# One decode step of attention plus FFN on one core: bias row, uneven last weight chunks, FFN behind attention, fewer K buffers

The chip is one Trainium2, the kernel runs on one NeuronCore. The metric is the device time of one execution in microseconds (us), median of several runs.

Names in what follows: PE multiplies matrices (PEld is the loading of its weights) and writes to PSUM; DVE and ACT are the vector and the scalar engine, POOL is GpSimd; SyncE (SP) issues loads; a q behind a name (SPq) marks what an engine's instruction queue does. A load has landed when the last of the 16 DMA engines has reported its share.

## The reference

For one token `x` (512 values) the kernel computes a layernorm, then two branches, and adds them to `x`:

```python
xn = layernorm(x)                                   # 1 x 512
q  = xn @ wq                                        # 512 x 4096: 32 heads of 128
k, v = last 1024 positions of the caches            # 32 heads x 1024 x 128, bf16
o  = softmax(q k^T * 128**-0.5) v
A  = o @ wo                                         # 4096 x 512
h  = relu(xn @ w1 + b1)**2                          # 512 x 1376
B  = h @ w2 + b2                                    # 1376 x 512
out = x + A + B
```

All of it is matrix times vector. K, V, wq, wo, w1 and w2 are read once, 27.99 MB in all by the page's count of reads, and nothing is used twice.

## The kernel before

SyncE issues all large loads in one queue, in the order wq, K, w1, w2, V, wo. ACT's queue takes the small ones. (Cuts are marked with `...`.)

```python
    b2T = const.tile([P, DJ], BF16, name="b2T")                    # P = 128, DJ = 4
    with nc.allow_non_contiguous_dma(reason="tiny b2 transpose load"):
        nc.scalar.dma_start(out=b2T[:], in_=B_b2.rearrange("(c p) -> p c", p=P))
    ...
    for g in range(NHG):                                           # 8 K tiles of 1 MB, then w1, w2, 8 V tiles
        kg = kvpool.tile([P, HG, NB, DH], BF16, name="kg", tag="k4", bufs=NHG)
        ...
    for q in range(NWC):                                           # 4 chunks of wo, 8 row blocks each
        woq = wpool.tile([P, JQ, D], BF16, name="woq", tag="w8k", bufs=NWC)
        nc.sync.dma_start(out=woq[:], in_=...)                     # rows of 512 bf16: 1 KB pieces
    ...                                                            # layernorm, then hT (FFN), q, K loop, softmax, V
    for q in range(NWC):
        ...
        for c in range(DJ):
            if q == 0: ...                                         # w2 matmuls into the same PSUM tile
            for jj in range(JQ):
                nc.tensor.matmul(oq[:, c:c + 1], lhsT=woq[:, jj, c * P:(c + 1) * P], rhs=oT_sb[:, j:j + 1], ...)
        ...                                                        # acc += oq, for q == 1 also acc += b2T
    nc.vector.tensor_copy(out=outT_bf[:], in_=acc[:])
    for c in range(DJ):
        nc.tensor.matmul(row_ps[0:1, c * P:(c + 1) * P], lhsT=outT_bf[:, c:c + 1], rhs=ident[:, :], start=True, stop=True)
    nc.vector.tensor_copy(out=out_sb[:], in_=row_ps[:])
    nc.scalar.dma_start(out=out[0, 0:1, :], in_=out_sb[:])
```

## Time and profile before

| | before |
|---|---|
| device time | 84.87 us (6 runs, 84.72 to 85.15) |
| span of the profiled run | 83.07 us |
| last byte of wo landed | 78.21 us |
| from there to the end of the span | 4.86 us |
| DMA queue of SyncE, share of the 16 engines | 93.0% |
| busiest compute engine | PE, 60% |

The span is what the profile covers; the device time is some 1.9 us longer. The way to read this table is: a stream of loads that never stops, then a short serial tail. The lines behind it stand in the prediction.

Two kinds of line need a key. A line of a timeline gives start and length in us, engine, line of the kernel, operation, output<-inputs, shapes and count; in brackets, how long the engine was idle before it and what ended that. A line of a stretch gives its bounds and length, the busy time of PE, PEld, DVE, ACT and POOL (with counts), the granted clock of PE (1.00 is full), the busy share of the DMA engines (above 1 where packets overlap) and GB/s.

### The profile page before, as it was taken

What the parts mean: (1) busy time and instruction counts of PE and PEld (TensorE: products, weight loads), DVE (VectorE), ACT (ScalarE), POOL (GpSimd) and SP (SyncE); (2) the same over time, 40 slices, a digit from 0 to 9 for tenths busy, and PEclk for the clock granted to TensorE, in tenths of its full rate; (3) what the DMA queues carried; (4) which work ended last, traced back from release to release, by engine and by line L of the source; (5) the groups of instructions that cost most, each with busy time, mean ns of one, the idle gap of its engine ahead of it and who ended that gap; (6) DMA issues with size and microseconds to landing.
All of it is one profiled execution on the core that took longest, in us unless ns stands there. A gap on an engine that the chain in (4) does not pass through costs nothing.

```text
span 83.1 us, 2488 instructions
## 1 busy us (share of the span) xinstructions
PE 50.2 (60%) x1149; PEld 45.3 (55%) x1149; DVE 20.5 (25%) x49; ACT 15.4 (19%) x17; POOL 0.8 (1%) x7
## 2 busy tenths in 40 slices
PE   0120001999898879896798929911791881564340
PEld 0120001999798768775697818901791871564320
DVE  0131000014533545363535620163100000020040
ACT  0634000004043144143440440014000000000000
POOL 4000000000000000000000000000000000000000
PEclk9999999999999999999999996555555555555555
DMA  2799998999999999999999999999999999999100
GB/s 28 320 427 407 406 351 257 400 398 388 387 390 387 383 388 388 387 394 386 353 360 386 387 389 379 387 387 387 390 384 380 363 348 347 350 348 293 61 8 0
DMA packets 15664, 28.15 MB, mean 339 GB/s; under 512 B 963, under 2 KB 6437, under 8 KB 15142
## 3 DMA queue, kind: packets, MB, share of 16 engines
q1 hardware_dynamic: 15008, 27.89, 93.0%
q10 hardware_dynamic: 646, 0.10, 0.8%
q8 instruction: 9, 0.15, 0.8%
q14 instruction: 1, 0.01, 0.0%
HBM read 27.99 MB, written 0.00 MB: 337 GB/s over the span
## 4 chain that ended last, share of the span: by engine, by line
PE 41%; DMA 29%; ACT 10%; DVE 9%; issue 7%; SPq 1%; ACTq 0%; DVEq 0%
DMA wqj<-in_A_wq_dram 14%; PE kt_ps L166 14%; DMA woq<-in_A_wo_dram 14%; ACT kT L169 9%; PE scT_ps L173 7%; PE oT_ps L204 7%; DVE kT L171 4%; PE qT_ps L155 4%; PE hT_ps L141 3%; DVE mx L182 1%; SPq L85 1%; ACT p_un L187 1%; PE hT_ps L138 1%; PE S_ps L180 1%; PE outQ L225 1%
## 5 line engine op out<-in xcount | busy, mean ns | idle before, releaser
L166 PE MATMUL kt_ps<-ident,kg 128*128 128x128 bf16 x256 | 22.1, 242 | 0.0
L171 DVE COPY kT<-kt_ps 128x1024 bf16<-128x1024 bf16 x21 | 14.0, 688 | 15.6 <-PE kt_ps L166 15.5
L166 PEld LDWEIGHTS <-kg 128*128 128x128 bf16 x256 | 17.4, 109 | 0.0
L169 ACT COPY kT<-kt_ps 128x1024 bf16<-128x1024 bf16 x11 | 11.1, 1012 | 30.5 <-PE kt_ps L166 28.4
L173 PE MATMUL scT_ps<-qT_sb,kT 128*128 128x1 bf16 x256 | 11.3, 166 | 4.5 <-ACT kT L169 3.5
L173 PEld LDWEIGHTS <-kT 128*128 128x128 bf16 x256 | 9.5, 100 | 7.2 <-ACT kT L169 4.6
L204 PE MATMUL oT_ps<-pT_sb,vg 128*128 128x1 bf16 x256 | 7.1, 165 | 2.5 <-issue 2.0
L155 PE MATMUL qT_ps<-xnT,wqj 128*128 128x1 bf16 x128 | 4.0, 165 | 7.5 <-DMA wqj<-in_A_wq_dram 5.9
L204 PEld LDWEIGHTS <-vg 128*128 128x128 bf16 x256 | 7.0, 104 | 2.7 <-issue 2.7
L225 PE MATMUL outQ<-oT_sb,woq 128*128 128x1 bf16 x128 | 4.5, 166 | 5.8 <-DMA woq<-in_A_wo_dram 4.2
L155 PEld LDWEIGHTS <-wqj 128*128 128x128 bf16 x128 | 3.7, 104 | 7.8 <-DMA wqj<-in_A_wq_dram 6.2
L225 PEld LDWEIGHTS <-woq 128*128 128x128 bf16 x128 | 4.0, 104 | 6.1 <-DMA woq<-in_A_wo_dram 4.4
L141 PE MATMUL hT_ps<-xnT,w_sb 128*128 128x1 bf16 (+1 forms) x44 | 3.1, 175 | 0.0
L138 PE MATMUL hT_ps<-one,b_row 1*128 1x1 bf16 (+1 forms) x11 | 2.0, 185 | 1.4 <-DMA b_row<-in_B_b_dram 1.4
L158 DVE CAST qT_sb<-qT_ps 128x32 bf16<-128x32 f32 x1 | 0.2, 191 | 10.1 <-PE qT_ps L155 10.1
L207 DVE CAST oT_sb<-oT_ps 128x32 bf16<-128x32 f32 x1 | 0.2, 192 | 9.4 <-PE oT_ps L204 9.4
L195 PE MATMUL pT_ps<-ident,p_rows 32*128 32x32 bf16 x8 | 0.4, 185 | 3.5 <-DVE p_rows L192 3.5
L187 ACT ACTIVATE p_un<-S_ps,negmx 32x1024 bf16<-32x1024 bf16 x1 | 1.1, 1105 | 7.0 <-DVE negmx L184 7.0
L141 PEld LDWEIGHTS <-w_sb 128*128 128x128 bf16 (+1 forms) x44 | 2.2, 112 | 0.2
L195 PEld LDWEIGHTS <-p_rows 32*128 32x128 bf16 x8 | 0.3, 100 | 3.7 <-DVE p_rows L192 3.7
L111 PE MATMUL xT_ps<-one,x_row 1*128 1x1 bf16 x4 | 0.3, 165 | 3.2 <-DMA x_row<-in_A_x_dram 3.2
L138 PEld LDWEIGHTS <-b_row 1*128 1x128 bf16 (+1 forms) x11 | 1.1, 103 | 1.6 <-DMA b_row<-in_B_b_dram 1.5
(45 smaller groups left out, 17.9 us busy)
## 6 DMA issues: line engine op xcount, KB each, us to landing
kg<-in_A_k_cache_dram SPq DMA_DIRECT2D x8, 1024.0 KB, 14.4
vg<-in_A_v_cache_dram SPq DMA_DIRECT2D x8, 1024.0 KB, 13.9
wqj<-in_A_wq_dram SPq DMA_DIRECT2D x4, 1024.0 KB, 7.6
woq<-in_A_wo_dram SPq DMA_DIRECT2D x4, 1024.0 KB, 12.8
w_sb<-in_B_w_dram SPq DMA_DIRECT2D x1, 1376.0 KB
w_sb<-in_B_w_dram SPq DMA_DIRECT2D x1, 1280.0 KB, 16.1
w_sb<-in_B_w_dram ACTq DMA_DIRECT2D x1, 96.0 KB, 7.0
x_row<-in_A_x_dram ACTq DMA_DIRECT2D x1, 1.0 KB
```

The costliest lines, as they stand in the source:

```text
L85: nc.sync.dma_start(out=wqj[:], in_=A_wq[j * P:(j + 1) * P, :])
L138: nc.tensor.matmul(hT_ps[0:M, t:t + 1], lhsT=b1_row[0:1, t * P:t * P + M], rhs=one11[0:1, 0:1], start=True, stop=False)
L141: nc.tensor.matmul(hT_ps[0:M, t:t + 1], lhsT=w1_sb[:, j, t * P:t * P + M], rhs=xnT[:, j:j + 1], start=False, stop=(j == DJ - 1))
L155: nc.tensor.matmul(qT_ps[:, h:h + 1], lhsT=wq_tiles[j][:, h * DH:(h + 1) * DH], rhs=xnT[:, j:j + 1], start=(j == 0), stop=(j == DJ - 1))
L166: nc.tensor.transpose(kt_ps[:, b, :], kg[:, hi, b, :], ident[:, :])
L169: nc.scalar.copy(out=kT[:], in_=kt_ps[:])
L171: nc.vector.tensor_copy(out=kT[:], in_=kt_ps[:])
L173: nc.tensor.matmul(scT_ps[:, b, h:h + 1], lhsT=kT[:, b, :], rhs=qT_sb[:, h:h + 1], start=True, stop=True)
L180: nc.tensor.transpose(S_ps[:, b * P:(b + 1) * P], scT_sb[:, b, :], ident[:, :])
L187: nc.scalar.activation(out=p_un[:], in_=S_ps[:], func=ACT.Exp, bias=negmx[:], scale=1.0, accum_out=ssum[:])
L204: nc.tensor.matmul(oT_ps[:, h:h + 1], lhsT=vg[:, hi, b, :], rhs=pT_sb[:, b, h:h + 1], start=(b == 0), stop=(b == NB - 1))
L225: nc.tensor.matmul(oq[:, c:c + 1], lhsT=woq[:, jj, c * P:(c + 1) * P], rhs=oT_sb[:, j:j + 1], start=first, stop=(jj == JQ - 1))
```

## The change

It follows the habits of someone tuning the end and the small loads: load b2 as one row and add it by a matmul; cut wo so that the last chunk is short; let the last add write bf16; copy the result on ACT and send it from SyncE; put the FFN behind attention in the source with its own PSUM tile; take six K buffers and three kT buffers to make room for the longer wo chunks.

```diff
-    NWC = 4
+    WO_CHUNKS = [10, 10, 9, 3]
+    NWBIG = 4
+    K_BUFS = 6
...
-    b2T = const.tile([P, DJ], BF16, name="b2T")
-    with nc.allow_non_contiguous_dma(reason="tiny b2 transpose load"):
-        nc.scalar.dma_start(out=b2T[:], in_=B_b2.rearrange("(c p) -> p c", p=P))
+    b2_row = const.tile([1, D], BF16, name="b2_row")
+    nc.scalar.dma_start(out=b2_row[:], in_=B_b2.rearrange("(o f) -> o f", o=1))
...                                   (hT, relu: moved from ahead of q to behind oT)
-        kT = work.tile([P, NB, P], BF16, name="kT", tag="kT", bufs=4)
+        kT = work.tile([P, NB, P], BF16, name="kT", tag="kT", bufs=3)
...
+    outB = psum.tile([P, DJ], F32, name="outB", tag="PH")          (w2 matmuls go here)
+    nc.vector.tensor_add(out=acc[:], in0=xcat[:, 0:DJ], in1=outB[:])
...
-    nc.vector.tensor_copy(out=outT_bf[:], in_=acc[:])
+        nc.vector.tensor_add(out=(outT_bf if last else acc)[:], in0=acc[:], in1=oq[:])
+    nc.tensor.matmul(row_ps[:, :], lhsT=one11[0:1, 0:1], rhs=b2_row[0:1, :], start=True, stop=False)
...
-    nc.vector.tensor_copy(out=out_sb[:], in_=row_ps[:])
-    nc.scalar.dma_start(out=out[0, 0:1, :], in_=out_sb[:])
+    nc.scalar.copy(out=out_sb[:], in_=row_ps[:])
+    nc.sync.dma_start(out=out[0, 0:1, :], in_=out_sb[:])
```

More of the change, by code (lines that the diff above doesn't have):

```diff
@@ L48 @@
     NOQ = HQ * DH // P
-    NWC = 4
-    JQ = NOQ // NWC
-    NDQ = DH // 32
-    assert NDQ * 32 == DH and HQ == 32
+    WO_CHUNKS = [10, 10, 9, 3]
+    NWBIG = 4
     KT_BUFS = 4
+    K_BUFS = 6
+    V_BUFS = 8
     const = ctx.enter_context(tc.tile_pool(name="const", bufs=1))
@@ L77, with bigdma @@
     nc.scalar.dma_start(out=w2_sb[0:FLAST, FT - 1, :], in_=B_w2[(FT - 1) * P:F, :])
-    b2T = const.tile([P, DJ], BF16, name="b2T")
-    with nc.allow_non_contiguous_dma(reason="tiny b2 transpose load"):
-        nc.scalar.dma_start(out=b2T[:], in_=B_b2.rearrange("(c p) -> p c", p=P))
+    b2_row = const.tile([1, D], BF16, name="b2_row")
+    nc.scalar.dma_start(out=b2_row[:], in_=B_b2.rearrange("(o f) -> o f", o=1))
+    qengines = [nc.sync]
+    qi = [0]
+    def bigdma(out_ap, in_ap):
+        eng = qengines[qi[0] % len(qengines)]
+        qi[0] += 1
+        eng.dma_start(out=out_ap, in_=in_ap)
     wq_tiles = []
     for j in range(DJ):
-        wqj = wpool.tile([P, HQ * DH], BF16, name="wqj", tag="w8k", bufs=NWC)
-        nc.sync.dma_start(out=wqj[:], in_=A_wq[j * P:(j + 1) * P, :])
+        wqj = wpool.tile([P, HQ * DH], BF16, name="wqj", tag="wbig", bufs=NWBIG)
+        bigdma(wqj[:], A_wq[j * P:(j + 1) * P, :])
         wq_tiles.append(wqj)
@@ L88 @@
     for g in range(NHG):
-        kg = kvpool.tile([P, HG, NB, DH], BF16, name="kg", tag="k4", bufs=NHG)
+        kg = kvpool.tile([P, HG, NB, DH], BF16, name="kg", tag="k4", bufs=K_BUFS)
         src = A_k_cache[0, g * HG:(g + 1) * HG, SK - W:SK, :].rearrange("h (p b) d -> p h b d", b=NB)
-        nc.sync.dma_start(out=kg[:], in_=src)
+        bigdma(kg[:], src)
         k_tiles.append(kg)
-    nc.sync.dma_start(out=w1_sb[:], in_=B_w1.rearrange("(j p) f -> p j f", p=P))
-    nc.sync.dma_start(out=w2_sb[:, 0:FT - 1, :],
-                      in_=B_w2[0:(FT - 1) * P, :].rearrange("(t p) n -> p t n", p=P))
+    bigdma(w1_sb[:], B_w1.rearrange("(j p) f -> p j f", p=P))
+    bigdma(w2_sb[:, 0:FT - 1, :], B_w2[0:(FT - 1) * P, :].rearrange("(t p) n -> p t n", p=P))
     v_tiles = []
     for g in range(NHG):
-        vg = kvpool.tile([P, HG, NB, DH], BF16, name="vg", tag="v4", bufs=NHG)
+        vg = kvpool.tile([P, HG, NB, DH], BF16, name="vg", tag="v4", bufs=V_BUFS)
         src = A_v_cache[0, g * HG:(g + 1) * HG, SK - W:SK, :].rearrange("h (p b) d -> p h b d", b=NB)
-        nc.sync.dma_start(out=vg[:], in_=src)
+        bigdma(vg[:], src)
         v_tiles.append(vg)
     wo_tiles = []
-    for q in range(NWC):
-        woq = wpool.tile([P, JQ, D], BF16, name="woq", tag="w8k", bufs=NWC)
-        nc.sync.dma_start(out=woq[:],
-                          in_=A_wo[q * JQ * P:(q + 1) * JQ * P, :].rearrange("(j p) n -> p j n", p=P))
-        wo_tiles.append(woq)
+    j0 = 0
+    for q, nj in enumerate(WO_CHUNKS):
+        if nj >= 8:
+            woq = wpool.tile([P, nj, D], BF16, name="woq", tag="wbig", bufs=NWBIG)
+        else:
+            woq = wpool.tile([P, nj, D], BF16, name="wolast", tag=f"wosmall{q}", bufs=1)
+        bigdma(woq[:], A_wo[j0 * P:(j0 + nj) * P, :].rearrange("(j p) n -> p j n", p=P))
+        wo_tiles.append((j0, nj, woq))
+        j0 += nj
+    assert j0 == NOQ
     xT_ps = psum.tile([P, DJ], F32, name="xT_ps", tag="PA")
@@ L133 @@
                             op0=ALU.subtract, op1=ALU.mult)
-    hT_ps = psum.tile([P, FT], F32, name="hT_ps", tag="PH")
-    for t in range(FT):
-        M = P if t < FT - 1 else FLAST
-        nc.tensor.matmul(hT_ps[0:M, t:t + 1], lhsT=b1_row[0:1, t * P:t * P + M], rhs=one11[0:1, 0:1],
-                         start=True, stop=False)
-        for j in range(DJ):
-            nc.tensor.matmul(hT_ps[0:M, t:t + 1], lhsT=w1_sb[:, j, t * P:t * P + M], rhs=xnT[:, j:j + 1],
-                             start=False, stop=(j == DJ - 1))
-    h_bf = work.tile([P, FT], BF16, name="h_bf")
-    h2 = const.tile([P, FT], BF16, name="h2")
-    nc.vector.tensor_copy(out=h_bf[:, 0:FT - 1], in_=hT_ps[:, 0:FT - 1])
-    nc.vector.scalar_tensor_tensor(out=h2[:, 0:FT - 1], in0=h_bf[:, 0:FT - 1], scalar=0.0, in1=h_bf[:, 0:FT - 1],
-                                   op0=ALU.max, op1=ALU.mult)
-    nc.vector.tensor_copy(out=h_bf[0:FLAST, FT - 1:FT], in_=hT_ps[0:FLAST, FT - 1:FT])
-    nc.vector.scalar_tensor_tensor(out=h2[0:FLAST, FT - 1:FT], in0=h_bf[0:FLAST, FT - 1:FT], scalar=0.0,
-                                   in1=h_bf[0:FLAST, FT - 1:FT], op0=ALU.max, op1=ALU.mult)
     qT_ps = psum.tile([P, HQ], F32, name="qT_ps", tag="PA")
@@ L207 @@
     nc.vector.tensor_copy(out=oT_sb[:], in_=oT_ps[:])
+    hT_ps = psum.tile([P, FT], F32, name="hT_ps", tag="PH")
+    for t in range(FT):
+        M = P if t < FT - 1 else FLAST
+        nc.tensor.matmul(hT_ps[0:M, t:t + 1], lhsT=b1_row[0:1, t * P:t * P + M], rhs=one11[0:1, 0:1],
+                         start=True, stop=False)
+        for j in range(DJ):
+            nc.tensor.matmul(hT_ps[0:M, t:t + 1], lhsT=w1_sb[:, j, t * P:t * P + M], rhs=xnT[:, j:j + 1],
+                             start=False, stop=(j == DJ - 1))
@@ new lines @@
+    h_bf = work.tile([P, FT], BF16, name="h_bf")
+    h2 = const.tile([P, FT], BF16, name="h2")
+    nc.vector.tensor_copy(out=h_bf[:, 0:FT - 1], in_=hT_ps[:, 0:FT - 1])
+    nc.vector.scalar_tensor_tensor(out=h2[:, 0:FT - 1], in0=h_bf[:, 0:FT - 1], scalar=0.0, in1=h_bf[:, 0:FT - 1],
+                                   op0=ALU.max, op1=ALU.mult)
+    nc.vector.tensor_copy(out=h_bf[0:FLAST, FT - 1:FT], in_=hT_ps[0:FLAST, FT - 1:FT])
+    nc.vector.scalar_tensor_tensor(out=h2[0:FLAST, FT - 1:FT], in0=h_bf[0:FLAST, FT - 1:FT], scalar=0.0,
+                                   in1=h_bf[0:FLAST, FT - 1:FT], op0=ALU.max, op1=ALU.mult)
@@ L209 @@
+    outB = psum.tile([P, DJ], F32, name="outB", tag="PH")
+    for c in range(DJ):
+        for t in range(FT):
+            Kt = P if t < FT - 1 else FLAST
+            nc.tensor.matmul(outB[:, c:c + 1], lhsT=w2_sb[0:Kt, t, c * P:(c + 1) * P], rhs=h2[0:Kt, t:t + 1],
+                             start=(t == 0), stop=(t == FT - 1))
     acc = const.tile([P, DJ], F32, name="acc")
-    out_tags = ["PA", "PB", "KT", "KT"]
-    for q in range(NWC):
+    nc.vector.tensor_add(out=acc[:], in0=xcat[:, 0:DJ], in1=outB[:])
@@ L212 @@
+    outT_bf = work.tile([P, DJ], BF16, name="outT_bf")
+    out_tags = ["PA", "PB", "KT", "KT", "KT", "KT"]
+    for q, (j0, nj, woq) in enumerate(wo_tiles):
         oq = psum.tile([P, DJ], F32, name=f"outQ{q}", tag=out_tags[q],
                        bufs=(KT_BUFS if out_tags[q] == "KT" else 1))
-        woq = wo_tiles[q]
         for c in range(DJ):
-            first = True
-            if q == 0:
-                for t in range(FT):
-                    Kt = P if t < FT - 1 else FLAST
-                    nc.tensor.matmul(oq[:, c:c + 1], lhsT=w2_sb[0:Kt, t, c * P:(c + 1) * P], rhs=h2[0:Kt, t:t + 1],
-                                     start=first, stop=False)
-                    first = False
-            for jj in range(JQ):
-                j = q * JQ + jj
-                nc.tensor.matmul(oq[:, c:c + 1], lhsT=woq[:, jj, c * P:(c + 1) * P], rhs=oT_sb[:, j:j + 1],
-                                 start=first, stop=(jj == JQ - 1))
-                first = False
@@ L228 @@
-        if q == 0:
-            nc.vector.tensor_add(out=acc[:], in0=xcat[:, 0:DJ], in1=oq[:])
-        else:
-            nc.vector.tensor_add(out=acc[:], in0=acc[:], in1=oq[:])
-        if q == 1:
-            nc.vector.tensor_add(out=acc[:], in0=acc[:], in1=b2T[:])
-    outT_bf = work.tile([P, DJ], BF16, name="outT_bf")
-    nc.vector.tensor_copy(out=outT_bf[:], in_=acc[:])
+            for jj in range(nj):
+                j = j0 + jj
+                nc.tensor.matmul(oq[:, c:c + 1], lhsT=woq[:, jj, c * P:(c + 1) * P], rhs=oT_sb[:, j:j + 1],
+                                 start=(jj == 0), stop=(jj == nj - 1))
@@ L237 @@
+        last = q == len(wo_tiles) - 1
+        nc.vector.tensor_add(out=(outT_bf if last else acc)[:], in0=acc[:], in1=oq[:])
     row_ps = psum.tile([1, D], F32, name="row_ps", tag="PA")
+    nc.tensor.matmul(row_ps[:, :], lhsT=one11[0:1, 0:1], rhs=b2_row[0:1, :], start=True, stop=False)
     for c in range(DJ):
         nc.tensor.matmul(row_ps[0:1, c * P:(c + 1) * P], lhsT=outT_bf[:, c:c + 1], rhs=ident[:, :],
-                         start=True, stop=True)
+                         start=False, stop=(c == DJ - 1))
```

## The prediction

> **What bounds the kernel now.** I read the page's slices first, then the busy time by stretch, then the tail of the timeline, then what the DMA queue of SyncE waited for.
>
> ```profile
> PE 50.2 (60%) x1149; PEld 45.3 (55%) x1149; DVE 20.5 (25%) x49; ACT 15.4 (19%) x17; POOL 0.8 (1%) x7
> ...
> DMA  2799998999999999999999999999999999999100
> GB/s 28 320 427 407 406 351 257 400 398 388 387 390 387 383 388 388 387 394 386 353 360 386 387 389 379 387 387 387 390 384 380 363 348 347 350 348 293 61 8 0
> ...
> q1 hardware_dynamic: 15008, 27.89, 93.0%
> q10 hardware_dynamic: 646, 0.10, 0.8%
> q8 instruction: 9, 0.15, 0.8%
> ```
>
> The DMA row is full from slice 2 to slice 36, and no compute engine comes near that: the kernel is one stream of 28.15 MB on SyncE's queue plus what has to follow its last byte. Only slices 5 and 6 dip (351, 257), and slices 36 and 37 run out unevenly (293, 61). In stretches (us, then busy times; the last two columns are DMA share and GB/s):
>
> ```profile
> 3.00:10.00 7.00, 1.35 (x9) 0.99 (x9) 1.25 (x7) 2.66 (x4) 0.00 (x0) 1.00 1.02 414
> 10.00:15.00 5.00, 1.05 (x33) 0.97 (x34) 0.00 (x0) 0.00 (x0) 0.00 (x0) 1.00 0.92 316
> 15.00:35.00 20.00, 18.42 (x370) 17.16 (x368) 7.61 (x12) 5.17 (x6) 0.00 (x0) 1.00 1.05 390
> 42.00:64.00 22.00, 14.73 (x338) 13.07 (x335) 6.40 (x15) 4.23 (x5) 0.00 (x0) 0.69 1.05 384
> 66.00:76.00 10.00, 5.65 (x195) 5.35 (x193) 0.67 (x4) 0.00 (x0) 0.00 (x0) 0.50 1.10 349
> ```
>
> The wq stage runs at 414, K and V at about 390, wo at 349; 10 to 15 us is the hole. The rest of the time is the tail:
>
> ```profile
> 78.26 1.01 PE L225 MATMUL outQ<-oT_sb,woq 128*128 128x1 bf16 x32 [1.73 <-DMA woq<-in_A_wo_dram]
> 79.31 0.16 DVE L231 TENSOR_TENSOR acc<-acc,outQ 128x4 f32<-128x4 f32 x1 [2.59 <-PE outQ L225]
> 79.50 0.17 DVE L235 CAST outT_bf<-acc 128x4 bf16<-128x4 f32 x1
> ...
> 79.72 0.58 PE L239 MATMUL row_ps<-ident,outT_bf 128*1 128x128 bf16 x4 [0.45 <-DVE outT_bf L235]
> 80.35 0.68 DVE L242 CAST out_sb<-row_ps 1x512 bf16<-1x512 f32 x1 [0.68 <-PE row_ps L239]
> 81.06 0.27 ACTq L243 DMA_DIRECT2D out_dram<-out_sb  x1
> ```
>
> The last wo bytes land at 78.21 us; everything after is a serial chain of 4.86 us to the span's end at 83.07. PE waits there, before 78.26, for a transfer. So only two things count: when the stream ends, and how long the chain behind it is.
>
> **What the Trainium skill says.** (1) "DMA: Bandwidth & Descriptors", § Rules for kernel authors: a strided last dimension "lowers to one descriptor per element". The trace agrees: the b2T load of 1 KB is 512 packets of 2 bytes on ACT's queue, most of q10's 646. It was issued at 1.93 and took 13.8 us to land. (2) The same page, § Queues, rings and completion order: each DMA engine takes turns between its queues, a packet at a time. Agrees: from 7.7 to 15.2 us the packet records show about as many 2-byte starts as starts of big packets (27 and 27 in the half microsecond from 8.5). (3) The same page, § Why small descriptors are slow: a fixed cost for each packet. The stretches agree: 8 KB packets 414, 2 KB about 390, 1 KB 349 GB/s. The wo rows stay 1 KB in the change, so its stage stays at 349. (4) "Runtime: NRT & Kernel Launch", § Instruction fetch mechanics: instructions come in 16 KiB blocks of 256 through a DMA queue. Agrees: q8 has 9 packets for 0.15 MB; each takes about 1.1 us of one DMA engine. PE stalls about 2 us in mid-loop at 62.66, with no data missing, after a block was requested at 62.32.
>
> **The change, part by part.**
>
> *b2 as one row instead of b2T.* Removes the 512 tiny packets. Their own time in the packet records is 4.6 us over 16 engines: 0.29 us each, nearly sure to come back. The hole they sit in is larger: from 10 to 15 us the stream moved 316 GB/s, while about 402 (the mean of 414 and 390) would have been normal: 5 x 86 = 430 KB, at 390 GB/s 1.1 us. What I can't settle is whether they cause it all. For it: the rate is clean as soon as they end (401 to 407 GB/s from 15.1 us), K packets of 84 ns took up to 372 ns while they ran, and later changes of tensor (35, 42, 64 us) show no such hole. Against: the same mixing from 8 to 10 us cost nothing (414 GB/s). I give 0.6 that the whole 1.1 us returns, 0.4 that only 0.3 does: mean 0.8 us.
>
> The load has a second effect: SyncE's queue reuses the semaphore of b2T for the fifth K tile and waits for it:
>
> ```profile
> SPq L91 <- DMA b2T<-in_B_b_dram: 2.4, 1, 2.4
> ```
>
> That issue slips from 13.37 to 15.79 us, but the four tiles issued before it are still queued (they land at 17.4, 20.1, 22.8 and 26.8 us), so I count nothing for it.
>
> *Chunks of wo, 10+10+9+3 instead of 8 each.* The bytes are the same, so the stream's end doesn't move. Behind it stand 12 matmuls, not 32. The trace starts one each 0.027 us and the last takes 0.165: 31 x 0.027 + 0.165 = 1.01 now, 11 x 0.027 + 0.165 = 0.47 after: 0.54 off the path. The chunk before lands 3/32 of 4.19 MB, 0.39 MB, earlier: 1.1 us at 349 GB/s. Its 36 matmuls need 36 x 0.027 = 0.97 us, so they're just out of the way.
>
> *Last add writes bf16 at once.* Takes the cast L235 away: 0.17 plus 0.02 of hop, 0.19. Adding b2 as a matmul into row_ps goes ahead of the last transfer: nothing on the path. *Output copy on ACT:* kT copies on ACT take 1.01 us for 1024 columns and a one-column operation there 0.20, so 512 cost about 0.6 against 0.68: 0.08 gained. *Output DMA from SyncE:* one more of the same kind; SyncE's issues take 0.37 or more where ACT's took 0.27: 0.05 to 0.1 lost. Tail in sum: 0.54 + 0.19 + 0.08 - 0.07 = about 0.75 us.
>
> *FFN moved behind attention.* Now its hT matmuls stand among the softmax's transposes on PE (49.9 to 53.4 us) and hold the softmax up by about 3.5 us. That isn't on the path: the last V tile lands only at 66.5. If the scheduler fills PE's idle time during the softmax with them (PE idles 3.5 us before pT), oT starts near 55 instead of 58.65 and waits for V anyway. Worth 0.
>
> *Six K buffers instead of eight, three kT instead of four.* The seventh K load now waits until the first tile is transposed (head 3 ends at 21.3 us; it was issued at 19.94), the eighth until head 7 (about 26; it was 23.51). The queue holds three to four tiles of 2.7 us each, so at 26 us some three are still ahead: no gap. kT with one buffer less may add a microsecond to the K loop, which has slack until V.
>
> Sum: 0.75 of tail, 0.8 of stream: 1.55 us. 84.87 - 1.55 = 83.3.
>
> **Rivals.** *A: the hole isn't the tiny packets* (a cold start of K, or the last wq tile). Then 0.75 + 0.3 = 1.05 us: 83.8. For it speaks the clean stretch 8 to 10. *B: the FFN runs late.* If its 99 matmuls stay behind oT in PE's order, then from 67.7: hT at 0.31 us per five is 3.4 us, a relu 0.8, the second product 44 x 0.027 = 1.2, the chunks of 10, 10 and 9 rows 3.2: ready at 76.3 without a fetch stall, 78 to 80 with one or two of 2 us. PE would become the bound, for 84 to 87 us. Against it: the order of the old kernel is not that of its source (the first hT matmul runs at 5.97, the rest at 50), so instructions go where PE is free, and the new PSUM tile for the second product doesn't depend on oT. I give it one in ten. *C: K buffers starve the stream.* Would show as a hole near 27 to 35 us worth 1 to 3 us; the queue's depth speaks against it. One in twenty. *D: the uneven end stays.* The last transfer's 16 engines finished from 76.4 to 78.2: half are late by the fetches of (4). The number of PE instructions barely changes, so I expect the same 1.8 us of run-out; it is neither gain nor loss.
>
> **Range and chances.** Two humps: 84.87 - 0.75 - 1.1 = 83.0 (0.55) and 83.8 (0.33), each with about 0.25 of spread, and a thin part above 84.5 (0.12, rivals B and C, in part mild). The mean of the first two lies near 83.3. Two per cent is 1.70 us, that is 83.17, which cuts the first hump: some 0.7 of it lies below, so 0.41 faster, 0.54 same, 0.05 slower. Eight in ten: 82.7 to 84.3.
>
> **What will show each step right or wrong.** The q10 line: some 130 packets, not 646. GB/s near 390 to 410 in slices 5 and 6, and the wo transfers' end at 77.1 (rival A: 77.9). 12 matmuls behind the last landing, then one add, the row matmuls, one ACT copy near 0.6; from landing to the span's end 4.1 instead of 4.86. hT matmuls in the gap before pT and outB before oT is done. No hole between 25 and 40 us. I would be wrong if PE isn't waiting for the last transfer at the end (B), if the stream shows a new hole (C), or if the dip stands with the tiny packets gone (A).

## The result, and the profile after

The changed kernel takes 82.84 us (8 runs, 82.61 to 82.92) against 84.88 (16 runs) before; the ratio is 0.9756, with a 95% interval of 0.9744 to 0.9767: faster by 2.4%. A ratio here compares the runs of both kernels in the same rounds, so it isn't quite the ratio of the medians quoted. All runs are fast: none is more than 1% above the fastest of its kernel.

The page of the changed kernel: DMA share and GB/s in forty slices, then ACT's queue (packets, MB, share).

```profile
DMA  2799999999999999999999999999999999999400
GB/s 29 311 418 417 421 429 376 388 384 385 390 386 386 384 387 388 390 394 393 354 364 383 388 388 382 387 386 387 387 381 384 365 353 349 348 356 342 142 8 1
...
q10 hardware_dynamic: 118, 0.10, 0.5%
```

The dip of slices 5 and 6 is gone (429 and 376 now, 351 and 257 before), and ACT's queue has 118 packets instead of 646. The slow start and the uneven run-out at the end are still there. By stretch (last column GB/s):

```profile
3.00:10.00 7.00, 1.36 (x9) 0.99 (x9) 1.25 (x7) 2.28 (x4) 0.00 (x0) 1.00 1.02 423
10.00:15.00 5.00, 1.51 (x51) 1.44 (x52) 0.00 (x0) 0.00 (x0) 0.00 (x0) 1.00 1.01 400
```

From 10 to 15 us the stream moves 400 instead of 316 GB/s, and from 3 to 10 us 423 instead of 414. The last byte of wo lands at 77.00 us, 1.21 earlier. The tail in the timeline:

```profile
77.05 0.48 PE L236 MATMUL outQ<-oT_sb,wolast 128*128 128x1 bf16 x12
...
77.56 0.16 DVE L239 TENSOR_TENSOR outT_bf<-acc,outQ 128x4 bf16<-128x4 f32 x1 [0.20 <-PE outQ L236]
...
77.78 0.59 PE L244 MATMUL row_ps<-ident,outT_bf 128*1 128x128 bf16 x4 [0.25 <-DVE outT_bf L239]
78.40 0.58 ACT L247 CAST out_sb<-row_ps 1x512 bf16<-1x512 f32 x1 [23.62 <-PE row_ps L244]
79.00 0.32 SPq L248 DMA_DIRECT2D out_dram<-out_sb  x1
```

From the landing to the span's end at 81.02 us it is 4.02 us, against 4.86. So 1.21 us of the stream and 0.84 of the tail make the 2.05 us by which the spans differ. Nothing else is left to explain in the total, but two things off the path changed and are worth reading. SyncE's queue now waits for PE before the seventh and eighth K load, and V's matmuls stall twice:

```profile
SPq L87 <- PE kt_ps L160: 5.7, 2, 3.5
```

```profile
55.85 1.33 PE L224 MATMUL outB<-h,w_sb 128*128 128x1 bf16 x44
...
57.04 2.83 PE L198 MATMUL oT_ps<-pT_sb,vg 128*128 128x1 bf16 x101
...
62.06 3.58 PE L198 MATMUL oT_ps<-pT_sb,vg 128*128 128x1 bf16 x128 [2.18 <-issue]
...
68.80 0.88 PE L198 MATMUL oT_ps<-pT_sb,vg 128*128 128x1 bf16 x27 [3.17 <-issue]
```

The first is harmless: slices 12 to 18 stay at 384 to 394 GB/s. The second brings the end of oT to 69.7 us, later than before (67.8), but the second wo chunk lands only at 72.77, so PE waits for transfers again from there on.

### The profile page after: what moved, and what is told of

It is laid out like the page before. It is cut to its first block, busy times and chain, and to the rows that moved or that the text cites.

```text
span 81.0 us, 2488 instructions
## 1 busy us (share of the span) xinstructions
PE 50.0 (62%) x1150; PEld 45.1 (56%) x1150; DVE 19.5 (24%) x47; ACT 16.0 (20%) x18; POOL 0.8 (1%) x7
## 2 busy tenths in 40 slices
DMA packets 15138, 28.15 MB, mean 347 GB/s; under 512 B 436, under 2 KB 5911, under 8 KB 14616
## 3 DMA queue, kind: packets, MB, share of 16 engines
q1 hardware_dynamic: 15010, 27.89, 94.6%
## 4 chain that ended last, share of the span: by engine, by line
SPq 46%; DMA 31%; PE 17%; issue 1%; DVE 1%; ACT 1%
SPq L87 46%; DMA woq<-in_A_wo_dram 17%; DMA wqj<-in_A_wq_dram 14%; PE kt_ps L160 8%; PE qT_ps L149 4%; PE outQ L236 2%; PE scT_ps L167 1%; DVE kT L165 1%; PE row_ps L244 1%; ACT out_sb L247 1%; DVE outT_bf L239 0%
## 5 line engine op out<-in xcount | busy, mean ns | idle before, releaser
L236 PEld LDWEIGHTS <-woq 128*128 128x128 bf16 x116 | 3.4, 104 | 4.1 <-DMA woq<-in_A_wo_dram 3.7
L236 PE MATMUL outQ<-oT_sb,woq 128*128 128x1 bf16 x116 | 3.6, 165 | 3.1 <-DMA woq<-in_A_wo_dram 2.8
L247 ACT CAST out_sb<-row_ps 1x512 bf16<-1x512 f32 x1 | 0.6, 576 | 23.6 <-PE row_ps L244 23.6
L239 DVE TENSOR_TENSOR acc<-acc,outQ 128x4 f32<-128x4 f32 x3 | 0.5, 158 | 7.0 <-PE outQ L236 7.0
```

The costliest lines, as they stand in the source:

```text
L247: nc.scalar.copy(out=out_sb[:], in_=row_ps[:])
```

## The experiments

Each kernel below gave the right result. The last column is the ratio to the kernel before, times 84.88 us, less the same product for the changed kernel (0.9756). The ratio is used because the rounds ran on different chips, on which the kernel before took 84.88 to 85.07 us. The intervals of the ratios are worth 0.12 to 0.27 us to either side.

| run | time, us | ratio to before (95%) | from the changed kernel, us |
|---|---|---|---|
| changed kernel | 82.84 | 0.9756 (0.9744 to 0.9767) | 0 |
| e1_b2row | 83.97 | 0.9881 (0.9856 to 0.9906) | +1.06 |
| e4_tail_only | 84.00 | 0.9895 (0.9874 to 0.9915) | +1.18 |
| e7_order_buffers | 85.01 | 1.0001 (0.9987 to 1.0016) | +2.08 |
| e5_even_chunks | 83.45 | 0.9807 (0.9785 to 0.9828) | +0.43 |
| e2_tiny_back | 83.98 | 0.9891 (0.9871 to 0.9911) | +1.15 |
| e6_tiny_half | 84.19 | 0.9892 (0.9876 to 0.9909) | +1.15 |
| e12_tiny_quarter | 84.33 | 0.9926 (0.9902 to 0.9950) | +1.44 |
| e13_tiny_same_queue | 84.32 | 0.9927 (0.9905 to 0.9950) | +1.45 |
| e3_tiny_late | 83.17 | 0.9792 (0.9768 to 0.9816) | +0.31 |
| e8_wait_alone | 82.94 | 0.9744 (0.9722 to 0.9766) | -0.10 |
| e9_w2_long_rows | 82.99 | 0.9744 (0.9723 to 0.9766) | -0.10 |
| e11_w2_alone | 82.27 | 0.9701 (0.9669 to 0.9732) | -0.47 |

### The change taken apart

**e1_b2row**: the kernel before with the b2 row alone.

```diff
-    b2T = ...  (two-byte load)
+    b2_row = ...  (one row)
-            nc.vector.tensor_add(out=acc[:], in0=acc[:], in1=b2T[:])
+    nc.tensor.matmul(row_ps[:, :], lhsT=one11[0:1, 0:1], rhs=b2_row[0:1, :], start=True, stop=False)
```

> The kernel before with only the b2 part of the change: b2 as one row, added by a matmul into row_ps. Theory (the 512 two-byte packets made the whole hole between 10 and 15 us): 10 to 15 us moves about 400 GB/s, the last wo bytes land near 77.0 instead of 78.2, tail unchanged but for one DVE add, time 84.88 - 1.2 = 83.7. Rival A (only their own 0.29 us): the hole stays, 84.6.

It gained 1.01 us (1 - 0.9881 of 84.88); the wo bytes landed at 77.07 us, and 10 to 15 us moved 397 GB/s:

```profile
10.00:15.00 5.00, 1.69 (x57) 1.61 (x58) 0.00 (x0) 0.00 (x0) 0.00 (x0) 1.00 1.00 397
```

The change of one 1 KB load is half of the whole gain. Rival A falls. The landing came 1.14 us earlier, more than the gain: in the profiled run the tail was 5.10 us instead of 4.86, as the last 32 matmuls took 1.26 us instead of 1.01.

**e4_tail_only**: the changed kernel with its b2 part undone.

```diff
-    b2_row = ...  (one row)
+    b2T = ...  (two-byte load)
-    nc.tensor.matmul(row_ps[:, :], lhsT=one11[0:1, 0:1], rhs=b2_row[0:1, :], start=True, stop=False)
+    nc.vector.tensor_add(out=acc[:], in0=acc[:], in1=b2T[:])
```

> The changed kernel without its b2 part (two-byte load kept and used by a DVE add): all else of the change. Theory: tail 4.0 us instead of 4.86, stream end still 78.2: 84.88 - 0.84 = 84.0. If the parts don't simply add up, the sum of this gain and that of the b2 part alone differs from 2.04 us.

It gained 0.89 us; the hole is there again (315 GB/s from 10 to 15 us) and the last landing was at 78.28, with 4.0 us behind it. The two gains, 1.01 and 0.89, make 1.90, against 2.07 for both: they add up within the intervals of some 0.2 us each.

**e7_order_buffers**: the kernel before with the two parts that were counted as zero.

```diff
-    (hT and relu ahead of q; w2 matmuls in the first wo tile)
+    (hT and relu behind oT; w2 matmuls in outB, added to xcat)
-        kg = ... bufs=NHG          kT = ... bufs=4
+        kg = ... bufs=6            kT = ... bufs=3
```

> The kernel before with only the two parts that were counted as worth nothing: the FFN's matmuls moved behind attention in the source (with their own PSUM tile), and six K and three kT buffers. Theory: 0, that is 84.9 within 0.2, with the stream ending at 78.2 as before and hT in the gap before pT. Rival (they carry part of the gain that the tail is credited with): 84.6 or less; rival C (the K buffers starve the stream): 85.3 or more.

85.01 us, ratio 1.0001: nothing, as expected. Moving 55 matmuls off the softmax's way buys no time in a kernel that waits for its last transfer, and two K buffers less cost none. So the gain of e4_tail_only is, by difference, the tail's.

**e5_even_chunks**: the changed kernel with four even wo chunks.

```diff
-    WO_CHUNKS = [10, 10, 9, 3]
+    WO_CHUNKS = [8, 8, 8, 8]
```

> The changed kernel with four even wo chunks of 8. Theory: the stream ends at 77.0 as before, 32 matmuls instead of 12 behind it: +0.54 us, 83.4. Rival (the short last chunk does nothing, since the chunk ahead of it keeps PE busy until then): +0.2 or less, 83.0.

Its timeline behind the last landing, at 76.98 us:

```profile
77.03 1.01 PE L236 MATMUL outQ<-oT_sb,woq 128*128 128x1 bf16 x32 [1.72 <-DMA woq<-in_A_wo_dram]
78.08 0.16 DVE L239 TENSOR_TENSOR outT_bf<-acc,outQ 128x4 bf16<-128x4 f32 x1 [2.58 <-PE outQ L236]
```

The last add starts 1.10 us behind the landing, in the changed kernel 0.56: 0.54 us, the predicted figure to the hundredth, and 0.43 in the time, which the interval allows.

### What about the two-byte load costs the time?

The load is dead in the next runs: it goes into a tile that nothing reads.

**e2_tiny_back**: the load put back into the changed kernel.

```diff
+    b2T = const.tile([P, DJ], BF16, name="b2T")
+    nc.scalar.dma_start(out=b2T[:], in_=B_b2.rearrange("(c p) -> p c", p=P))
```

> The changed kernel with the old two-byte load of b2 put back, into a tile that nothing reads. Theory: the hole returns and with it 1.1 to 1.2 us: 84.0. Rival A: 0.3 us, 83.1. Rival (the hole went because of the other parts of the change): 82.84.

+1.15 us, and the hole is back:

```profile
10.00:15.00 5.00, 1.04 (x33) 0.96 (x34) 0.00 (x0) 0.00 (x0) 0.00 (x0) 1.00 0.94 318
```

The load itself is the cause; nobody has to use it. One side effect has to be kept apart. This kernel, e6 and e12 have one DMA more than the changed kernel, and in them it is the fourth K load that SyncE's queue holds back until b2T has landed:

```profile
SPq L90 <- DMA b2T<-in_B_b_dram: 6.6, 1, 6.6
```

In e6 it is 4.7 us, in e12 2.3. The stream behind shows no hole from it (393, 391 and 391 GB/s from 15 to 25 us), and the next run tests such a wait, on the fifth load, without the two-byte load.

**e8_wait_alone**: no load, but the fifth K load held back as it was before.

```diff
+        if g == 4:
+            nc.gpsimd.tensor_copy(out=kg[:, 0, 0, 0:4], in_=k_tiles[0][:, 0, 0, 0:4])
         bigdma(kg[:], src)
```

> The changed kernel with the fifth K load held back until the first K tile has landed (GpSimd copies 4 columns of it into the fifth tile first), so near 16.5 us instead of 12.6: a little later than the 15.8 at which the kernel before issued it after its wait for b2T. No two-byte packets. If the hole came from this wait and not from the packets: +1 us or more, 83.9, with a hole between 13 and 17 us. Theory: the queue holds enough, 82.84 within 0.2.

The issue slipped to 16.47 us and SyncE's queue shows a wait of 3.9 us for it, yet the time is that of the changed kernel and the stream shows no hole:

```profile
10.00:15.00 5.00, 1.65 (x56) 1.57 (x57) 0.00 (x0) 0.00 (x0) 0.00 (x0) 1.00 1.00 398
15.00:20.00 5.00, 5.00 (x113) 5.00 (x110) 1.02 (x3) 1.01 (x1) 0.19 (x1) 1.00 1.05 386
```

So the wait of 2.4 us for b2T, which the change removes, was worth nothing, and what counted is the load.

**e6_tiny_half** and **e12_tiny_quarter**: half and a quarter of the load, 256 and 128 packets.

```diff
+        nc.scalar.dma_start(out=b2T[:, 0:2], in_=B_b2.rearrange("(c p) -> p c", p=P)[:, 0:2])     # half
+        nc.scalar.dma_start(out=b2T[:, 0:1], in_=B_b2.rearrange("(c p) -> p c", p=P)[:, 0:1])     # quarter
```

> The changed kernel with half of the two-byte load put back (256 packets, dead tile); taken one for each 8 KB packet from 7.7 us on they should be over near 12 us, before K starts at 12.6. If each packet costs the same: half of the full load's price, 0.6 us, 83.4. If the hole needs two-byte packets while K starts: 0.3 or less, 83.1.

> The changed kernel with a quarter of the two-byte load put back (128 packets, one for each partition, dead tile). Half of the load cost as much as all of it, so the price isn't one for each packet. If it is one for the load as such while wq runs in 8 KB packets: about 1.1 us again, 83.9. If it falls with the count below half: 83.1 to 83.4.

Both theories of e6 were wrong. Half of the packets cost as much as all (+1.15 us), a quarter no less (+1.44). The holes only move. The stretch of the half load, then two of the quarter:

```profile
8.00:13.00 5.00, 0.37 (x2) 0.21 (x2) 0.00 (x0) 0.00 (x0) 0.00 (x0) 1.00 0.83 311
8.00:11.50 3.50, 0.18 (x1) 0.10 (x1) 0.00 (x0) 0.00 (x0) 0.00 (x0) 1.00 0.68 258
11.50:14.00 2.50, 0.19 (x1) 0.10 (x1) 0.00 (x0) 0.00 (x0) 0.00 (x0) 1.00 1.00 421
```

The quarter's DMA share of 0.68 shows engines standing idle while the load runs, though all four wq loads had been issued by 2.8 us, and the rate is clean as soon as it is over, well before K starts. In the half load the hole lies between 8 and 13 us. So the hole doesn't need the start of K, and its price isn't one for each packet: 128 packets cost what 512 do.

**e13_tiny_same_queue**: all 512 packets, but issued by SyncE behind wq.

```diff
+    nc.sync.dma_start(out=b2T[:], in_=B_b2.rearrange("(c p) -> p c", p=P))      # after the four wq loads
```

> The changed kernel with the full two-byte load put back, but issued by SyncE behind the wq loads, so that it stands in the same queue as the big packets and doesn't take turns with them. If the turns between two queues make the hole: only the packets' own time, 0.3 us, 83.1. If two-byte packets as such stall an engine: 1.1 us or more, 83.9.

```profile
8.00:12.50 4.50, 0.37 (x2) 0.21 (x2) 0.00 (x0) 0.00 (x0) 0.00 (x0) 1.00 1.01 423
12.50:14.50 2.00, 0.90 (x34) 0.91 (x35) 0.00 (x0) 0.00 (x0) 0.00 (x0) 1.00 0.38 88
14.50:20.00 5.50, 4.86 (x120) 4.78 (x117) 0.88 (x2) 0.35 (x1) 0.00 (x0) 1.00 1.05 398
```

+1.45 us, as one clean gap: 423 GB/s, then 88 for 2 us, then 398 again. So turn-taking between two queues isn't needed for the cost. K's first load had been issued at 5.59 us, so the gap isn't a want of work. The packets ran from 12.7 to 14.7 us; if they are spread evenly, an engine got through its 32 in about 2 us, some 60 ns each (an estimate), although each record says 9 ns: here the busy time of a tiny packet leaves out most of what it costs the stream.

**e3_tiny_late**: all 512 packets on ACT's queue, but only once q is ready.

```diff
+    nc.vector.tensor_copy(out=b2T[:], in_=qT_sb[:, 0:DJ])       # holds the load back
+    nc.scalar.dma_start(out=b2T[:], in_=B_b2.rearrange("(c p) -> p c", p=P))
```

> As the run with the load put back, but it is issued only after qT_sb (about 17 us), so that it mixes with a steady stream of 2 KB K packets, and not with 8 KB packets or with the start of K. If every two-byte packet costs its neighbours time wherever it falls: +1.1 us, 84.0. If it costs only its own 9 ns: +0.3, 83.1. If the hole needs the passage from wq to K: at most +0.3.

+0.31 us. The packets ran from 21.2 to 25.1 us among K packets of 2 KB:

```profile
17.00:21.00 4.00, 4.00 (x57) 3.99 (x55) 2.06 (x5) 1.01 (x1) 0.00 (x0) 1.00 1.05 387
21.00:24.50 3.50, 3.25 (x45) 3.07 (x43) 1.25 (x3) 1.01 (x1) 0.00 (x0) 1.00 1.08 352
```

352 instead of 387 GB/s for 3.5 us is 122 KB, 0.32 us at 387 GB/s: as measured, and close to the packets' own busy time (5.5 us over 16 engines, 0.35). The same load costs 0.3 us here and 1.15 to 1.45 us when it runs in the wq stage or at its end. Why is left open. The neighbours of the dear variants were 8 KB packets or the first K packets; and what stays the same in all of them, while the number of packets falls to a quarter, is that they write to 128 partitions (as the cheap one does too). Which of these sets the price no run here separates.

### A better version

**e9_w2_long_rows**, then **e11_w2_alone**: both take w2 so that a partition holds ten neighbouring rows, with the hidden units permuted alike in w1 and b1.

```diff
-    bigdma(w2_sb[:, 0:FT - 1, :], B_w2[0:(FT - 1) * P, :].rearrange("(t p) n -> p t n", p=P))
+    bigdma(w2_sb[:, 0:FT - 1, :], B_w2[0:(FT - 1) * P, :].rearrange("(p t) n -> p t n", p=P))
+        fs = slice(t, (FT - 1) * P, FT - 1) if t < FT - 1 else slice(t * P, t * P + M)
-        ... lhsT=b1_row[0:1, t * P:t * P + M] ... lhsT=w1_sb[:, j, t * P:t * P + M]
+        ... lhsT=b1_row[0:1, fs] ...              lhsT=w1_sb[:, j, fs]
-    WO_CHUNKS = [10, 10, 9, 3]          (e9 only)
+    WO_CHUNKS = [10, 9, 9, 3, 1]
```

> An attempt at a better version: the changed kernel with w2 loaded so that each partition takes ten neighbouring rows (10 KB in one piece instead of ten of 1 KB; the hidden units are permuted alike in w1 and b1 by a stride), and wo in chunks of 10, 9, 9, 3, 1. If packet size sets the rate: 1.31 MB at about 420 instead of 349 GB/s saves 0.6 us, and 4 matmuls instead of 12 behind the last bytes 0.2: 82.0. If the rate has another cause: 82.6. If the strided weights slow hT down it is hidden before oT and costs nothing.

e9 missed: 82.99 us. Its w2 stage was faster (424 and 443 GB/s in slices 18 and 19, 393 and 354 in the changed kernel), w2 landing 3.12 us behind w1 instead of 3.60. But in its profiled run (82.73 us, the fastest of the four) the stream moved 217 GB/s from 2 to 4 us instead of 299, so wq ran some 0.5 us late and the gain was gone. The fifth chunk gave little: behind the landing it took 3.89 us instead of 4.02. Two short adds on DVE, one after the other, took the place of the matmuls saved, and 0.06 of the 0.13 us is a shorter sending of the output.

> The changed kernel with only the long rows of w2 (wo chunks as in the change). In the combined run the w2 stage became 0.5 us shorter but the start of the wq stage 0.5 us longer. If that late start was this one execution's: 82.84 - 0.5 = 82.35. If it comes with this kernel every time: 82.8, and the profile shows the wq tiles landing 0.5 us late again.

Without the fifth chunk: 82.27 us, ratio 0.9701 (0.9669 to 0.9732), 0.47 us better than the change and 3% better than before. From 39 to 43 us, where w2 ends, the stream moves 389 instead of 360 GB/s, and wo's last byte lands at 76.40. Four of its six runs took 82.19 to 82.31, two 82.87 and 82.93. In its profiled run wq started in time (287 GB/s from 2 to 4 us). Whether the two slow runs had e9's late start can't be seen, as only profiled runs leave a trace; what sets that start is open.

## Why the prediction was right, and what it had wrong

The measured 82.84 us lies inside 82.7 to 84.3, near the lower end. It came from the hump that was given 0.55, whose figure was 83.0. The class was not called: the prediction held "same" for likelier than "faster" (0.54 to 0.41), as 83.0 lies close to the 2% line at 83.17, and two terms that were each some 0.1 us too small put the result clearly on the other side. Step by step:

- **Bound.** Right. The time is the stream's end plus the tail: 77.00 + 4.02 us, predicted 77.1 + 4.1.
- **b2.** The whole hole came back, as the prediction gave 0.6 for. The size was slightly low, 1.1 for 1.21 us: 10 to 15 us gave 1.05 (84 GB/s more for 5 us, at 400), and 3 to 10 us, not counted, another 0.15 (423 for 414). Whether the packets cause this second part isn't shown: e7, with all of them, moved 422 GB/s from 8 to 10 us, as the changed kernel does. The clean stretch that spoke against the theory was read rightly, but it didn't bear on the hole: in the kernel before, the load cost little up to 10 us and much from 13 to 14 us (187 GB/s). If turns between queues were the mechanism in mind, they aren't needed: the price is there without them (e13), and it doesn't follow the number of packets (e6, e12).
- **SyncE's wait for b2T.** Counted as nothing; e8 shows that.
- **Tail.** 0.54 for the chunk, 0.19 for the cast: both exact. The copy on ACT took 0.58 us instead of 0.68 and saved 0.11 with its hop (the gap to the next instruction), predicted 0.08. Sending from SyncE was to lose 0.05 to 0.1 and lost 0.01: from issue to the span's end 2.02 us, before 2.01. Sum 0.84 for 0.75 (0.83 from these rounded parts). Only the chunk was changed alone (e5); the other parts are read off the timelines.
- **FFN and buffers.** Worth 0, as e7 shows. The details differ: hT ran in the gap before pT, but its conversion on DVE stood ahead of `negmx`, so the softmax still waited (53.58 us for the exponential) and oT started at 57.04, not near 55. It didn't matter, for the reason given.
- **Rival B** didn't happen; PE's stalls, read as instruction fetches, are larger than I allowed for (2.18 and 3.17 us), so a kernel with less slack between V and wo would have felt it. **Rival C** didn't either. **D** held: the last transfer's engines finished from 75.35 to 77.00, a spread of 1.65 us (1.79 before). The trace bears out its reason and more. By then eight instruction blocks had been fetched, and eight of the 16 engines finished 1.3 us or more behind the first; at the second wo chunk it was seven and seven. In both kernels, from the first block at 19 to 20 us on, the number of late engines (0.95 us or more behind the first) equals the number of blocks fetched so far for all but three of the loads: an engine that fetched a block seems to stay behind to the end. No run changes the number of blocks, so this is a reading of the traces, not a test.
- **Readings.** Two figures were misread, and neither carries the argument: 28.15 MB are all DMA packets, of which SyncE's queue moved 27.89; and the third K tile had landed on 15 of its engines at 22.8 us, on the last at 24.1.
- **The centre, 83.3,** was an average of two humps, with 0.33 given to rival A. Of the 0.46 us of the miss 0.2 are terms too small (0.11 in the stream, 0.09 in the tail); the rest is that hedge.

## What to carry to other kernels

In a kernel bound by one stream of loads, look at the GB/s line for holes before looking at any engine, and at what else was loading there: a 1 KB bias loaded element by element cost 1.0 to 1.2 us, more than all the rest of the change brought, and asking for fewer elements didn't help, while a row or a later moment did. Behind the last byte, make the last chunk short enough that the chunk ahead of it is just done; going on to a fifth chunk gave 0.13 us at most, since each chunk brings its own add. Matmuls moved (e7) or a queue's wait removed (e8) ahead of the last byte were worth nothing here, however large they look in the lists of waits, as long as the stream showed no hole for them.

## What the Trainium skill lacked or had wrong

- "DMA: Bandwidth & Descriptors", § Rules for kernel authors, says that a strided last dimension makes one descriptor per element. It lacks what this costs a stream beside it: 1.15 us for 512 packets of 2 bytes in the wq stage and the start of K, 1.15 for 256, 1.44 for 128, 1.45 in the stream's own queue, 0.31 later among 2 KB packets. No page was found that explains why the price doesn't follow the count.
- The same page, § Why small descriptors are slow, puts the overhead at about 3 bus cycles of 32 bytes a packet, and 32 bytes of descriptor besides. That would leave 32/36 = 0.89 of the full rate for 1 KB, 64/68 = 0.94 for 2 KB and 256/260 = 0.98 for 8 KB, so 0.90 and 0.96 of the 8 KB rate (an estimate from these figures). The runs show more loss: 349 and 387 GB/s against 423 for 8 KB packets, 0.83 and 0.91. The three rates fit 27.3 bytes per ns and engine plus some 9.5 ns a packet (an estimate from them). They come from different tensors, but w2 shows the same: 393 and 354 GB/s in the two slices of its 1 KB pieces, 424 and 443 when it came in pieces of 10 KB (e9).
- "Runtime: NRT & Kernel Launch", § Instruction fetch mechanics, calls the crossing of a 16 KiB block mostly hidden. With matmuls starting every 0.027 us it isn't: PE stood 2.18 and 3.17 us in the middle of V's matmuls. That these are fetches is inferred: both stops come at the same places in six traces looked at, before the 863rd and the 991st matmul, 128 matmuls and 128 weight loads apart, with a block on its way at 59.44 and 66.06 us. The page also lacks what a block costs the loads: each takes about 1.1 us on one DMA engine, and here the engines ended the last transfer up to 1.65 us apart.
